# Moving weights in the expert blocks and four dense output buffers, in a fused attention and mixture-of-experts kernel

## The chip, the cores and the metric

The kernel runs on one core of one Trainium2 chip, in one launch. The metric is the time on the device in microseconds (us). The kernel before the change took 663.98 us, the median of three runs (662.36 to 671.49).

A core has engines with instruction streams of their own: TensorE (PE in the profile, with its weight loads shown as PEld), VectorE (DVE), ScalarE (ACT), GpSimd (POOL) and SyncE (SP). They meet through semaphores. TensorE multiplies a *stationary* operand, loaded beforehand, with a *moving* operand that streams through the array, and writes to PSUM; other engines copy results from PSUM to SBUF. Transfers between SBUF and device memory run on DMA queues, which SyncE, ScalarE or GpSimd issue.

## What is computed

The reference in short, with the shapes of this case:

```python
# attention: q, k, v are [8, 8, 576, 64]
rel = pos[:, None] - pos[None, :]
scores = q @ k.T / 8 + slopes[h] * -abs(rel)         # ALiBi
scores = where((rel >= 0) & (rel < 128), scores, -1e9)
attn = softmax(scores)
x = (attn @ v)                                        # as [4608, 512]: 8 batches x 576 tokens
# mixture of experts on x
y_dense = relu(x @ w1_dense) @ w2_dense               # all weights 512 x 512
logits = x @ w_gate                                   # 8 experts
e = argmax(logits); gate = softmax(logits)[e]
y_moe = gate * (relu(x @ w1[e]) @ w2[e])              # one expert for each token
out = y_dense + y_moe                                 # [4608, 512], float32
```

## The kernel before

The program is one list of steps `n`. In the first 48 steps it does attention, three steps for each unit of one batch and four heads. Three steps behind, the attention rows are transposed (`flip`); then come the gate and the dense layer of each batch. Each token's row (x in bf16, its gate weight, its token number) is scattered to `xs_dram`, sorted by expert, and its dense result to `ys_dram`. From step 50 on, 43 *expert blocks* of 128 rows each load such rows back, apply the expert's two layers, add the dense result and scatter to `out`.

The order within a step is the order in which the engines get their instructions:

```python
while jm < NB:
    for f in gates.pop(n, []): f()          # gate_a, gate_b, gate_c, gate_d, routing
    lo = scores(u, pr)                      # TensorE scores, ScalarE exponentials p32
    if n - 2 in norms: norms.pop(n - 2)()   # VectorE: normalize, xf and xrow
    flip(*steps[n - 3])                     # TensorE transposes tp; ScalarE copies xT, xTb
    ...                                     # what is due later is put into gates and items
    for f in todo[:1]: f()                  # one item of the dense layer
    norms[n - 1] = attend(*steps[n - 1])    # TensorE: p @ v
    for f in todo[1:]: f()                  # the other items
    ...                                     # loads and casts of the next q, k, v
    lo()                                    # VectorE: low parts of p
    if n > NS + 1: block(jm); jm += 1
    n += 1
```

`tp`, `lp` (gate), `lg`, `pc`, `hp` and `yp` (dense) all take turns in one pair of PSUM buffers, with the tag `misc` in the pool `psum_m`. The dense layer:

```python
def dense1(b, c, hf):                       # hf: half of the 576 tokens, 288 each
    hp = psum_m.tile([P, 512], F32, name="hp", tag="misc")
    ...                                     # 4 matmuls of 288 columns
    nc.scalar.activation(out=hT[...], in_=hp[:, 0:HF], func=ACT.Relu)

def dense2(b, t):                           # t: one of five tiles of tokens
    yp = psum_m.tile([P, 512], F32, name="yp", tag="misc")
    ...                                     # 4 matmuls of 512 columns
    yt = xpool.tile([P, DM], F32, name="yt", tag="yt")     # xpool: 2 buffers
    nc.scalar.copy(out=yt[:rows, :], in_=yp[:rows, :])
    nc.gpsimd.indirect_dma_start(out=ys_dram[:, :], ..., in_=yt...)
```

The expert blocks:

```python
def fetch(j):                               # xr, yr: 4 buffers each
    ...                                     # SyncE loads xr from xs_dram, yr from ys_dram
def turn_x(j):
    ...                                     # 4 transposes of xr into xps; VectorE copies to xT
def layer1(j):
    hp = psum_h.tile([P, 4, P], F32, name="hpm", tag="hpm")
    for c in range(4):
        for kc in range(4):                 # weights stationary, 128 tokens moving
            nc.tensor.matmul(out=hp[:, c, :],
                lhsT=w_all[:, bass.DynSlice(er, 1), 0, kc, c * P : c * P + P],
                rhs=xT[:, kc, :], start=(kc == 0), stop=(kc == 3))
    nc.scalar.activation(out=hT, in_=hp, func=ACT.Relu)
def layer2(j):
    for c in range(4):                      # hT stationary, 512 weight columns moving
        nc.tensor.matmul(out=y, lhsT=hT[:, c, :],
            rhs=w_all[:, bass.DynSlice(er, 1), 1, c, :], start=(c == 0), stop=(c == 3))
    nc.vector.scalar_tensor_tensor(out=yo, in0=y, scalar=xr[:, GC : GC + 1], in1=yr,
        op0=ALU.mult, op1=ALU.add)          # gate weight times y, plus the dense result
    nc.gpsimd.indirect_dma_start(out=out[:, :], ..., in_=yo[:, :])   # token numbers from xr
def block(j):
    if j == 0: turn_x(0); layer1(0); turn_x(1)
    layer1(j + 1); turn_x(j + 2); layer2(j); fetch(j + 4)
```

## Time and profile before

The profile is of one execution with a span of 669.2 us.

| | busy us | share of the span | instructions |
|---|---|---|---|
| TensorE matmuls | 492.8 | 74% | 4378 |
| TensorE weight loads | 287.9 | 43% | 4424 |
| VectorE | 286.2 | 43% | 567 |
| ScalarE | 241.3 | 36% | 412 |
| GpSimd | 148.2 | 22% | 193 |

The mean granted clock of TensorE was 0.832 of full speed; 83.03 MB went through the DMA queues, 124 GB/s on average.

The lines in the prediction come from these views. *Stretches*: for each stretch of time, its length, then the busy time of each engine with the number of its instructions, the granted clock, the share of the DMA engines' time and their rate. *Waits*: who waited for whom, the sum in us, how many times, and the longest. An engine name with q is the engine's queue, such as SPq for SyncE's. *Timeline*: start, duration, engine, line of the kernel, operation and tiles (written <- read), and in brackets how long the engine was idle before, and what ended that.

L numbers are lines of the kernel: L373 and L384 are the scores, L394 the exponentials, L447 attend, L463 the normalization, L497 the copies xT and xTb, L513 the gate's matmuls, L642 and L649 the dense first layer and its ReLU, L658, L666 and L667 the dense second layer, its copy yt and its scatter, L845 the loads of a block, L860 and L866 the transposes xps and their copy, L881 and L889 the expert's first layer and its ReLU, L897 the second layer, L905 its sum, L913 the scatter to out.

### The profile page before, as it was taken

The page shows a single profiled execution, that of the slowest core. Times are in us where ns is not written, and L with a number is a line of the kernel's source. Part 1 is how long each engine was busy: PE and PEld are TensorE (multiplying, and loading weights), DVE is VectorE, ACT ScalarE, POOL GpSimd, SP SyncE. Part 2 cuts the span into 40 slices and gives each one's busy share as a digit, 9 for nine tenths or more (in the row PEclk, how much of TensorE's full clock was granted, in tenths as well). Part 3 has the DMA queues.
Part 4 walks back from the last instruction along what each step waited for, and adds up shares of the span by engine and source line. Part 5 has one row for each costly group of instructions (what it writes and reads, how often), then busy time and mean ns, then how long its engine had stood idle before and what let it go on. Part 6 is the DMA issues. An engine that isn't in the chain of part 4 may idle for free.

```text
span 669.2 us, 12798 instructions
## 1 busy us (share of the span) xinstructions
PE 492.8 (74%) x4378; PEld 287.9 (43%) x4424; DVE 286.2 (43%) x567; ACT 241.3 (36%) x412; POOL 148.2 (22%) x193
## 2 busy tenths in 40 slices
PE   1454877577677787675766687798877999999994
PEld 0343564254354454343534455344433444544442
DVE  4675764464563563644716744021142222222221
ACT  2433754463563563453635644221210111111110
POOL 4000012313303303213213212213411121222221
PEclk9996868787887887987968988797877787787887
DMA  8635663616636535625444121523474443444340
GB/s 171 161 109 140 149 144 100 189 38 158 189 61 153 164 75 132 171 66 144 110 129 104 19 85 41 162 79 103 160 227 151 149 128 113 132 126 142 122 147 21
DMA packets 87695, 83.03 MB, mean 124 GB/s; under 512 B 43603, under 2 KB 74323, under 8 KB 87636
## 3 DMA queue, kind: packets, MB, share of 16 engines
q1 hardware_dynamic: 69560, 48.76, 25.5%
q0 software_dynamic: 17680, 33.12, 19.6%
q8 instruction: 41, 0.67, 0.4%
q10 hardware_dynamic: 396, 0.33, 0.2%
q14 instruction: 18, 0.15, 0.1%
HBM read 64.79 MB, written 28.66 MB: 140 GB/s over the span
## 4 chain that ended last, share of the span: by engine, by line
issue 32%; PE 20%; DMA 18%; ACT 8%; POOL 8%; DVE 7%; another core or an unknown queue 3%; SPq 2%; POOLq 1%; ACTq 0%; DVEq 0%
DMA ys_dram<-yt,slot 11%; POOL out_dram L913 5%; PE hpm L881 4%; DMA qraw<-in_q_dram 4%; PE sq L373 3%; ACT p L394 3%; POOL xs_dram L599 3%; PE hp L642 3%; DVE plo L413 2%; PE sq L384 2%; PE lp L513 2%; DMA vf<-in_v_dram 2%; PE y L897 1%; ACT yt L666 1%
## 5 line engine op out<-in xcount | busy, mean ns | idle before, releaser
L881 PE MATMUL hpm<-xTm,w_all 128*128 128x128 bf16 x688 | 137.2, 240 | 12.0 <-DVE xTm L866 4.2
L413 DVE TENSOR_TENSOR plo<-p 128x1024 bf16<-128x1024 f32 (+1 forms) x96 | 82.9, 905 | 99.7 <-ACT p L394 99.1
L881 PEld LDWEIGHTS <-w_all 128*128 x688 | 68.9, 106 | 91.9 <-issue 33.3
L394 ACT ACTIVATE p<-sq 128x1024 f32<-128x1024 f32 (+1 forms) x96 | 69.2, 775 | 66.0 <-PE sq L384 65.9
L447 PE MATMUL ax<-vf,p 128*128 128x65 bf16 (+1 forms) x576 | 72.1, 212 | 26.2 <-DVE xf L463 26.2
L889 ACT ACTIVATE hTm<-hpm 128x512 bf16<-128x512 f32 x43 | 25.7, 597 | 174.7 <-PE hpm L881 174.7
L447 PEld LDWEIGHTS <-p 128*128 128x128 bf16 (+1 forms) x1152 | 70.1, 112 | 36.1 <-DVE xf L463 28.1
L866 DVE COPY xTm<-xps 128x512 bf16<-128x512 bf16 x43 | 18.2, 424 | 145.8 <-PE xps L860 136.9
L913 POOL DMA_INDIRECT out_dram<-yo,xr x43 | 42.1, 979 | 173.8 <-DVE yo L905 159.0
L447 PE MATMUL ax<-vf,plo 128*128 128x65 bf16 (+1 forms) x576 | 71.3, 209 | 2.8 <-DVE plo L413 2.8
L642 PE MATMUL hp<-xTb,w_all 128*128 128x288 bf16 x256 | 48.1, 317 | 34.1 <-ACT xTb L497 32.6
L447 PE MATMUL ax<-vl,p 128*128 128x64 bf16 (+1 forms) x576 | 71.5, 208 | 1.1 <-DVE vl L195 1.1
L667 POOL DMA_INDIRECT ys_dram<-yt,slot x40 | 41.6, 1040 | 112.1 <-ACT yt L666 107.4
L513 PE MATMUL lp<-xT,wg_pad 128*32 128x288 f32 x128 | 31.0, 585 | 45.4 <-ACT yt L666 21.8
L447 PEld LDWEIGHTS <-plo 128*128 128x128 bf16 (+1 forms) x576 | 61.9, 111 | 4.4 <-DVE plo L413 4.4
L897 PE MATMUL y<-w_all,hTm 128*128 x154 | 58.2, 502 | 1.9 <-issue 1.1
L658 PE MATMUL yp<-w_all,hTd 128*128 128x512 bf16 (+1 forms) x147 | 43.6, 408 | 19.6 <-ACT yt L666 13.1
L373 PE MATMUL sq<-mask,ident_b 128*128 128x512 bf16 (+1 forms) x177 | 47.9, 395 | 12.0 <-DVE mask L249 9.3
L649 ACT ACTIVATE hTd<-hp 128x288 bf16<-128x288 f32 x64 | 27.2, 425 | 72.0 <-remote 44.9
L599 POOL DMA_INDIRECT xs_dram<-xrow,slot x40 | 38.4, 961 | 61.4 <-DVE xrow L591 51.3
L905 DVE SCALAR_TENSOR_TENSOR yo<-y,xr,yr 128x512 f32<-128x512 f32 x43 | 32.3, 750 | 38.5 <-PE y L897 36.0
L666 ACT COPY yt<-yp 128x512 f32<-128x512 f32 (+1 forms) x40 | 23.6, 591 | 68.7 <-DMA ys_dram<-yt,slot 55.1
(139 smaller groups left out, 560.8 us busy)
## 6 DMA issues: line engine op xcount, KB each, us to landing
yr<-ys_dram SPq DMA_DIRECT2D x43, 256.0 KB
kraw<-in_k_dram SPq DMA_DIRECT2D x16, 576.0 KB
qraw<-in_q_dram SPq DMA_DIRECT2D x66, 128.0 KB
vf<-in_v_dram SPq DMA_DIRECT2D x64, 128.0 KB
w_all<-in_moe_w_dram POOLq DMA_DIRECT2D x16, 512.0 KB
xr<-xs_dram SPq DMA_DIRECT2D x43, 130.0 KB
ys_dram<-fill_y SPq DMA_DIRECT2D x8, 256.0 KB
xs_dram<-fill_x SPq DMA_DIRECT2D x8, 130.0 KB
```

The lines of the kernel that those rows point to most:

```text
L373: nc.tensor.matmul(out=sq[g // 2][:, g % 2, 0:tot], lhsT=ident_b, rhs=rhs, start=True, stop=False,)
L394: nc.scalar.activation(out=p32[:, :, 0:tot], in_=sq[i][:, :, 0:tot], func=ACT.Exp, scale=SCALE,)
L413: nc.vector.tensor_tensor(out=plo[:, :, 0:tot], in0=p32[:, :, 0:tot], in1=phi[:, :, 0:tot], op=ALU.subtract,)
L447: nc.tensor.matmul(out=ax[:rows, i, o0 : o0 + w], lhsT=lhs, rhs=rhs, start=(n == 1), stop=(n == 3 * len(kl)),)
L513: nc.tensor.matmul(out=lp[r0 : r0 + 32, 0:HF], lhsT=wg_pad[:, 2 * (u % HQ) + c, :], rhs=cur["xT"][:, c, hf * HF : (hf + 1) * HF], start=Tr ...
L599: ins = nc.gpsimd.indirect_dma_start(out=xs_dram[:, :], out_offset=bass.IndirectOffsetOnAxis(ap=slot[:rows, t : t + 1], axis=0), in_=xrow. ...
L642: nc.tensor.matmul(out=hp[:, 0:HF], lhsT=w_all[:, E, 0, kc, c * P : c * P + P], rhs=xTb[:, kc, hf * HF : hf * HF + HF], start=(kc == 0), s ...
L658: nc.tensor.matmul(out=yp[:rows, :], lhsT=hT[:, c, t * P : t * P + rows], rhs=w_all[:, E, 1, c, :], start=(c == 0), stop=(c == 3),)
L667: ins = nc.gpsimd.indirect_dma_start(out=ys_dram[:, :], out_offset=bass.IndirectOffsetOnAxis(ap=slots[b][:rows, t : t + 1], axis=0), in_=y ...
L881: nc.tensor.matmul(out=hp[:, c, :], lhsT=w_all[:, bass.DynSlice(er, 1), 0, kc, c * P : c * P + P], rhs=xT[:, kc, :], start=(kc == 0), stop ...
L897: nc.tensor.matmul(out=y, lhsT=hT[:, c, :], rhs=w_all[:, bass.DynSlice(er, 1), 1, c, :], start=(c == 0), stop=(c == 3),)
L913: ins = nc.gpsimd.indirect_dma_start(out=out[:, :], out_offset=bass.IndirectOffsetOnAxis(ap=xr.bitcast(I32)[:, TC : TC + 1], axis=0), in_= ...
```

## The change

It has these parts.

- **Expert blocks**: in the first layer x becomes the stationary operand and the weights move, 512 columns at a time. The result then has the tokens on the partitions, so that the gate weight can be applied in the ReLU as a scale for each row (it is positive, and the second layer is linear), and h must be transposed for the second layer (`turn_h`). It is meant to need fewer instructions on TensorE.
- **Dense output**: `yt` has four buffers. The dense layer runs in two token parts, tiles 0 and 1 (256 tokens), then tiles 2 to 4 (320 tokens), each through both layers, so that `hTd` is smaller.
- **Transposes first**: `flip` comes ahead of the scores in each step. The gate's matmuls become items beside the dense ones, and the gate's later parts are due a step or more earlier.
- **Space**: `fill_y` goes (the padding rows of `ys_dram` are filled from `fill_x`, in two pieces for each row instead of four), the constant `ut_f` takes a buffer of the probabilities, `ge` is bf16.

The core of the diff; cuts are marked with dots.

```diff
-    def gate_a(u):
+    def gate_a(u, hf):
...
-        for hf in range(2):
-            lp = psum_m.tile([P, 512], F32, name="lp", tag="misc")
+        lp = psum_m.tile([P, 512], F32, name="lp", tag="misc")
...
+    DT = [(0, 2), (2, NT)]
+
     def dense1(b, c, hf):
-        HF = S // 2
+        c0, c1 = DT[hf][0] * P, min(DT[hf][1] * P, S)
+        HF = c1 - c0
...
-        yt = xpool.tile([P, DM], F32, name="yt", tag="yt")
+        yt = xpool.tile([P, DM], F32, name="yt", tag="yt", bufs=4)
...
-        return [one[0:2], one[2:4], one[4:6], one[6:8], two[0:2], two[2:5]]
+        return [one[0:2], one[2:4], two[0:2], one[4:6], one[6:8], two[2:5]]
...
-        hp = psum_h.tile([P, 4, P], F32, name="hpm", tag="hpm")
+        hp = psum_h.tile([P, FF], F32, name="hpm", tag="hpm")
+        for kc in range(4):
+            nc.tensor.matmul(
+                out=hp,
+                lhsT=xT[:, kc, :],
+                rhs=w_all[:, bass.DynSlice(er, 1), 0, kc, :],
+                start=(kc == 0),
+                stop=(kc == 3),
+            )
+        hr = mpool.tile([P, FF], BF16, name="hr", tag="hr")
+        nc.scalar.activation(out=hr, in_=hp, func=ACT.Relu, scale=xr[:, GC : GC + 1])
+        st[("g", j)] = (hr, er)
+
+    def turn_h(j):
+        hr, er = st.pop(("g", j))
+        hps = psum_t.tile([P, 4, P], BF16, name="hps", tag="xps")
         for c in range(4):
-            for kc in range(4):
-                nc.tensor.matmul(
...
+            nc.tensor.transpose(
+                out=hps[:, c, :], in_=hr[:, c * P : (c + 1) * P], identity=ident_b
+            )
         hT = mpool.tile([P, 4, P], BF16, name="hTm", tag="hTm")
-        nc.scalar.activation(out=hT, in_=hp, func=ACT.Relu)
+        nc.scalar.copy(out=hT, in_=hps)
...
-        nc.vector.scalar_tensor_tensor(
-            out=yo, in0=y, scalar=xr[:, GC : GC + 1], in1=yr, ...
+        nc.vector.tensor_tensor(out=yo, in0=y, in1=yr, op=ALU.add)
...
             turn_x(1)
+        turn_h(j)
         if j + 1 < NB:
             layer1(j + 1)
...
-            for f in gates.pop(n, []):
-                f()
+            if 0 <= n - 3 < NS:
+                flip(*steps[n - 3])
+                ...                         # gate_a and gate_b, gate_c become items
             lo = None
             if n < NS:
                 u, pr = steps[n]
                 lo = scores(u, pr)
             if n - 2 in norms:
                 norms.pop(n - 2)()
-            if 0 <= n - 3 < NS:
-                flip(*steps[n - 3])
-                ...
+            for f in gates.pop(n, []):
+                f()
```

## The prediction

> **What bounds the kernel now.** I read the busy times by stretches first, because one average over 669 us hides that the program has two halves: attention with gates and dense layer (to about 427 us), then 43 expert blocks.

> ```profile
> core 0: us, PE busy (x) PEld busy (x) DVE busy (x) ACT busy (x) POOL busy (x), PEclk, DMA share, GB/s
> ...
> 200.00:250.00 50.00, 37.55 (x420) 23.44 (x424) 25.93 (x48) 25.72 (x44) 13.44 (x15) 0.81 0.52 131
> ...
> 520.00:560.00 40.00, 38.41 (x200) 19.51 (x202) 9.83 (x17) 5.37 (x9) 7.82 (x8) 0.80 0.40 125
> ```

> One batch of attention lasts about 51 us (step starts in the timeline: 184.2, 235.1, 288.7). TensorE works in 37.55 of 50 us there: a quarter is waiting, so the waits decide that half. In the expert stretch TensorE works in 38.41 of 40 us while VectorE, ScalarE and the transfers stay under half: TensorE alone decides there. The waits view says what the attention half waits for:

> ```profile
> ACT yt L666 <- DMA ys_dram<-yt,slot: 55.1, 21, 4.9
> ACT hTd L649 <- remote: 44.9, 7, 7.2
> PE hp L642 <- ACT xTb L497: 32.6, 26, 2.5
> ...
> PE lp L513 <- ACT yt L666: 21.8, 11, 4.5
> ...
> PE lp L513 <- ACT hTd L649: 17.6, 5, 4.5
> ...
> PE yp L658 <- ACT yt L666: 13.1, 6, 2.6
> ```

> ScalarE cannot empty a dense result, because both yt buffers still feed scatters (55.1 us). TensorE then finds no free PSUM buffer of the pair named misc: 21.8 + 13.1 us. It also waits 32.6 us for the copies xTb, which stand behind the exponentials on ScalarE. The chain of waits agrees: it puts 11% of the span on the dense scatter, its largest transfer share. For the other half, two expert blocks in the timeline:

> ```profile
> 561.16 0.98 POOL L913 DMA_INDIRECT out_dram<-yo,xr  x1 [4.21 <-DVE yo L905]
> ...
> 562.62 0.38 PE L860 MATMUL xps<-ident_b,xr 128*128 128x128 bf16 x4
> ...
> 562.88 0.60 ACT L889 ACTIVATE hTm<-hpm 128x512 bf16<-128x512 f32 x1 [4.22 <-PE hpm L881]
> 563.04 0.42 DVE L866 COPY xTm<-xps 128x512 bf16<-128x512 bf16 x1 [2.16 <-PE xps L860]
> ...
> 563.74 3.71 PE L881 MATMUL hpm<-xTm,w_all 128*128 128x128 bf16 x16
> 563.91 0.75 DVE L905 SCALAR_TENSOR_TENSOR yo<-y,xr,yr 128x512 f32<-128x512 f32 x1 [0.44 <-PE y L897]
> 564.00 0.33 SPq L845 DMA_DIRECT2D xr<-xs_dram  x1
> ...
> 564.93 0.98 POOL L913 DMA_INDIRECT out_dram<-yo,xr  x1 [2.79 <-DVE yo L905]
> ```

> The 16 first-layer matmuls take 3.71 us even at full clock (the windows view has 1.00 there): 0.224 us from start to start, though each moves 128 columns. A second-layer matmul moves 512 columns and starts every 0.215 us at full, every 0.427 us at half clock. The first layer is bound by the issuing of four instructions for each matmul (two address computations, weight load, matmul), not by the array. From the 11th output scatter (512.55) to the 42nd (659.84) lie 31 blocks of 4.75 us.

> [...] Here the clock does change in steps of 3.41 us, but it falls to 0.50 in stretches where the windows view has TensorE busy 1.00. [...] Here the next xr load starts 1.86 us after the scatter instruction before it ended (562.14 to 564.00).

> **The change, part by part.**

> *Expert blocks, TensorE.* Removed per block: 16 weight loads and 16 matmuls with the weights stationary, 3.6 us by the spacing above. Added: 4 matmuls that move 512 columns, 4 x 0.215 = 0.86 us, and 4 transposes, 0.38 us as for xps. A block is then 0.38 (hps) + 0.86 (layer 1) + 0.38 (xps) + 0.86 (layer 2) = 2.5 us at full clock. [...] I expect the clock near 1.0 in this stage.

> *Expert blocks, the other engines.* ScalarE gets a second evacuation: 0.60 + about 0.60 = 1.2 us a block. VectorE's output loses its multiplication and becomes a plain sum, 0.69 us as for the same shape at L463. Both stay under half of any period below. The new round trip (layer 1, ReLU, transpose, copy, layer 2) spans two steps: between hps and layer 2 TensorE has 0.86 + 0.38 us, against 0.60 plus some 0.3 of signals.

> *Expert blocks, the loop through memory.* There are still four xr buffers, and one is refilled only when its output scatter has landed:

> ```profile
> SPq L845 <- DMA out_dram<-yo,xr: 89.3, 28, 4.6
> ```

> From the timeline: output sum to scatter start 563.91 to 564.93, 1.02 us; scatter start to the next xr load 561.16 to 564.00, 2.84; that load to its last packet 564.00 to 565.68, 1.68, and up to 2.5 when it meets the yr load; then the transposes and layer 2 to the next output sum, 0.38 + 0.86 + 0.2. Together 7.0 to 7.8 us. The transposes run two blocks ahead and there are four buffers, so this is the length of two periods: a period is at least 3.5 to 3.9 us. Today's 4.75 hides it; with 2.5 us of TensorE it becomes the bound. I take 3.7: 31 x (4.75 - 3.7) = 33 us saved.

> *First blocks (427 to 512 us).* Ten blocks run there between the last batch's gates and dense layer, and one gap: TensorE waits 5.0 us for xr while SyncE issues the padding writes. TensorE bound, each block is worth 3.6 - 1.24 = 2.4 us less; but the loop limits them too and the gap stays. I take 20 us.

> *Dense layer.* Four yt buffers, with the scatters in groups of two and three and two steps between the groups, leave no scatter to wait for: of 21.8 + 13.1 = 35 us of TensorE idle time nearly all goes. The two parts of 256 and 320 tokens move the same columns as two of 288.

> *Transposes first.* xT and xTb are copied ahead of the exponentials, while TensorE still makes the scores. Of 32.6 us I expect two thirds, 22 us, to go; the gate's first half now follows its transposes closely and will wait in their stead. Against this I set 5 us of new waits. Attention: 35 + 22 - 5 = 52 us.

> *The rest* (no fill_y, a bf16 ge, the mask constant in a probability buffer) is off the path: under 0.5 us.

> Sum: 33 + 20 + 52 = 105 us, of which I keep 102, for three stages that can't all pay fully. 664 - 102 = 562 us.

> **Rivals.** (a) *TensorE alone still bounds the blocks*: 2.5 us at full clock, or 3.0 at today's 0.82. Then 31 x 2 = 62 us instead of 33, and about 530 us in all. Against it speaks the loop above, which no part of the change shortens by more than 0.1 us. (b) *The round trip over ScalarE becomes the bound*: if transposes wait for the ReLU in each step, a block is about 4.3 us; the stage then gives 14 us and the total is near 585. For it: xps and hps share one pair of PSUM buffers. Against: the order of instructions leaves 1.2 us of other TensorE work in each of the two waits. (c) *The attention waits are only exchanged.* Without the scatter waits a batch is 42 to 44 us; transfers, at a share of 0.52 today, would go to about 0.61, and the first 100 us show 0.60 to 0.64 with waits for q. Also the 44.9 us of hTd (a source that the profile does not tell; it falls together with the scatter of xs) stay. If half of the 52 us come back, the total is near 590. (d) *The dense scatters were hidden anyway*: the chain of waits has them with 11%, so I give this little.

> **Range and chances.** Attention alone may give 20 to 65 us, the blocks with their start 35 to 85. Both at their low end: about 609; both high: 514; neither corner is likely, and the estimate lies nearer to the good end of attention. I take 535 to 602. Every part of the sum points the same way and the threshold of 2% is 13 us, so faster 0.96, same 0.03, slower 0.01.

> **What would show it.** In the new profile: waits of yt for the ys_dram scatter near zero, and xTb waits a third of 32.6; batches of 42 to 44 us; blocks of 3.7 us, with TensorE busy under 80% of that stage, clock above 0.95, and TensorE or its loads waiting for the DMA of xr. If the blocks are shorter than 3.3 us, my loop is wrong; if they stay above 4.2 with waits for ScalarE, rival b is right; if the batches stay above 47 us, rival c. What would make the total wrong most easily is the attention half, where I removed waits one by one although each may uncover another.

## The result and the profile after

The changed kernel took **537.9 us** (537.49 to 539.59, three runs) against 663.98: a ratio of 0.8076 with a 95% interval of 0.7997 to 0.8156, 126 us less. The prediction of 562.0 had counted on 102; the result lies inside its range, near the fast end. How the 126 us are made up differs from the sum.

The windows view cuts both kernels at the first scores of the second and of the sixth batch, so each line holds four whole batches of attention, with the same 1,680-odd recorded TensorE matmuls. Before, then after, then after in the expert stretch; the columns are the stretch, its length, each engine's busy time, the granted clock, the share of the transfers, and GB/s:

```profile
core 0: us, PE busy (x) PEld busy (x) DVE busy (x) ACT busy (x) POOL busy (x), PEclk, DMA share, GB/s
106.90:314.90 208.00, 145.79 (x1682) 92.05 (x1696) 106.62 (x189) 106.63 (x186) 52.42 (x62) 0.82 0.50 126
```
```profile
101.70:248.30 146.60, 127.76 (x1687) 82.76 (x1697) 107.37 (x189) 106.81 (x185) 57.44 (x63) 0.97 0.73 181
...
450.00:490.00 40.00, 26.62 (x159) 13.15 (x161) 11.17 (x20) 12.73 (x20) 9.84 (x10) 0.91 0.49 152
```

A batch went from 208.0 / 4 = 52.0 us to 36.7. TensorE's idle time fell from 62.2 us in four batches to 18.8, 10.8 us less in each. But its *busy* time fell as well, by 18.0 / 4 = 4.5 us a batch for the same work, and the clock rose from 0.82 to 0.97. The prediction has nothing for that, and so its batches of 42 to 44 us were too long. In the expert stretch TensorE is now busy 26.6 of 40 us.

The waits view after, by total, count and longest:

```profile
PEld L864 <- DMA xr<-xs_dram: 70.5, 34, 8.4
...
PE hp L647 <- ACT hTd L654: 6.9, 9, 1.1
...
PE lp L510 <- DVE sl L585: 5.1, 6, 1.0
...
PE tp L488 <- ACT yt L670: 3.6, 5, 1.0
...
PE tp L488 <- ACT hTd L654: 3.3, 7, 0.5
...
PE hp L647 <- ACT xTb L495: 0.3, 1, 0.3
```

The waits of TensorE for yt (21.8 + 13.1 us before) have shrunk to 3.6, those for xTb (32.6) to 0.3, and that of hTd for an untold source (44.9) is not in the view at all (2.7 us of the kind are left at other tiles); nor is there a wait of yt for the scatter to `ys_dram` (55.1). The new ones sum to about 19 us, the yt wait included. At the top stands the wait that the prediction named for the blocks: the transposes' weight load, waiting for xr.

Two blocks of the timeline after show the loop through memory:

```profile
450.41 0.69 DVE L920 TENSOR_TENSOR yo<-y,yr 128x512 f32<-128x512 f32 x1 [0.44 <-PE y L912]
...
451.38 0.98 POOL L921 DMA_INDIRECT out_dram<-yo,xr  x1 [3.67 <-DVE yo L920]
...
454.23 0.33 SPq L849 DMA_DIRECT2D xr<-xs_dram  x1
...
456.32 0.23 PEld L864 LDWEIGHTS <-xr 128*128 128x128 bf16 x4 [1.48 <-DMA xr<-xs_dram]
456.33 0.40 PE L864 MATMUL xps<-ident_b,xr 128*128 128x128 bf16 x4 [0.99 <-DMA xr<-xs_dram]
...
456.56 1.03 PE L912 MATMUL y<-w_all,hTm 128*128 x4
...
457.63 0.69 DVE L920 TENSOR_TENSOR yo<-y,yr 128x512 f32<-128x512 f32 x1 [0.44 <-PE y L912]
```

Sum to scatter 0.97 us, scatter to the next load of its buffer 2.85, load to transposes 2.09, transposes to the output sum two blocks on 1.31: 7.22 us for two periods. This turn is one of the shortest. Over 27 turns in that trace the means are 0.97, 3.49, 2.24 and 1.40, together 8.1 us. From the 11th output scatter (402.2) to the 42nd (525.6) a block takes 123.4 / 31 = 3.98 us.

### The profile page after: what moved, and what is told of

It is laid out like the page before. It is cut to its first block, busy times and chain, and to the rows that moved or that the text cites. A ratio compares the mean times of both kernels' runs of the same rounds, so it can differ in the third digit from the quotient of the medians.

```text
span 535.8 us, 11040 instructions
## 1 busy us (share of the span) xinstructions
PE 378.4 (71%) x4043; PEld 228.6 (43%) x4080; DVE 283.1 (53%) x566; ACT 271.3 (51%) x455; POOL 158.0 (29%) x193
## 3 DMA queue, kind: packets, MB, share of 16 engines
q0 software_dynamic: 17680, 33.12, 24.3%
## 4 chain that ended last, share of the span: by engine, by line
PE 30%; issue 25%; DVE 16%; ACT 8%; DMA 8%; POOL 7%; SPq 3%; POOLq 1%; another core or an unknown queue 0%; DVEq 0%; ACTq 0%
PE ax L445 7%; DVE plo L411 7%; POOL out_dram L921 7%; PE hp L647 4%; PE yp L662 4%; DMA vf<-in_v_dram 4%; PE sq L382 3%; ACT p L392 3%; PE lp L510 3%; PE sq L371 2%; DVE xf L461 2%; PE tp L488 2%; ACT qT L182 2%; SPq L167 2%; DVE qs L175 2%
## 5 line engine op out<-in xcount | busy, mean ns | idle before, releaser
L870 DVE COPY xTm<-xps 128x512 bf16<-128x512 bf16 x43 | 18.2, 424 | 123.4 <-PE xps L864 106.7
L904 ACT COPY hTm<-hps 128x512 bf16<-128x512 bf16 x43 | 25.2, 586 | 88.3 <-PE hps L900 86.7
L864 PE MATMUL xps<-ident_b,xr 128*128 128x128 bf16 x172 | 18.6, 236 | 54.0 <-DMA xr<-xs_dram 54.0
L885 PE MATMUL hpm<-w_all,xTm 128*128 x162 | 48.5, 417 | 5.1 <-DVE xTm L870 3.6
L912 PE MATMUL y<-w_all,hTm 128*128 x167 | 47.4, 406 | 4.4 <-ACT hTm L904 3.9
L647 PE MATMUL hp<-xTb,w_all 128*128 128x256 bf16 (+1 forms) x256 | 42.1, 293 | 11.7 <-ACT hTd L654 6.9
L371 PE MATMUL sq<-mask,ident_b 128*128 128x512 bf16 (+1 forms) x183 | 39.6, 327 | 11.4 <-DVE mask L249 9.2
L893 ACT ACTIVATE hr<-hpm,xr 128x512 bf16<-128x512 f32 x43 | 29.6, 687 | 27.7 <-PE hpm L885 20.2
L864 PEld LDWEIGHTS <-xr 128*128 128x128 bf16 x172 | 12.0, 105 | 74.1 <-DMA xr<-xs_dram 70.5
L920 DVE TENSOR_TENSOR yo<-y,yr 128x512 f32<-128x512 f32 x43 | 29.7, 691 | 22.8 <-PE y L912 22.8
L654 ACT ACTIVATE hTd<-hp 128x256 bf16<-128x256 f32 (+1 forms) x64 | 26.1, 412 | 23.7 <-PE hp L647 19.8
```

The source lines that it names most:

```text
L371: nc.tensor.matmul(out=sq[g // 2][:, g % 2, 0:tot], lhsT=ident_b, rhs=rhs, start=True, stop=False,)
L647: nc.tensor.matmul(out=hp[:, 0:HF], lhsT=w_all[:, E, 0, kc, c * P : c * P + P], rhs=xTb[:, kc, c0:c1], start=(kc == 0), stop=(kc == 3),)
L864: nc.tensor.transpose(out=xps[:, kc, :], in_=xr.bitcast(BF16)[:, kc * P : (kc + 1) * P], identity=ident_b,)
L885: nc.tensor.matmul(out=hp, lhsT=xT[:, kc, :], rhs=w_all[:, bass.DynSlice(er, 1), 0, kc, :], start=(kc == 0), stop=(kc == 3),)
L912: nc.tensor.matmul(out=y, lhsT=hT[:, c, :], rhs=w_all[:, bass.DynSlice(er, 1), 1, c, :], start=(c == 0), stop=(c == 3),)
```

## The experiments

They ran in three sets, each set on one chip. The kernel before took 668.6, 630.5 and 631.3 us beside them, so the chips aren't alike and differences are taken within a set where possible. The theories: the blocks are bound by the loop of refills (L); in attention the dense buffers and the order of transposes each took away waits (W), and the faster clock came on top (C). The rivals are those of the prediction, and each expectation says what its letters stand for where they differ.

### Set 1 (before: 668.63 us): parts undone one at a time

**Two dense output buffers.** In the changed kernel:

```diff
-        yt = xpool.tile([P, DM], F32, name="yt", tag="yt", bufs=4)
+        yt = xpool.tile([P, DM], F32, name="yt", tag="yt", bufs=2)
```

> The changed kernel with two yt buffers instead of four; all else as changed. Theory W (the waits for the dense scatters were what the four buffers removed): in the new item order only the last tile of each batch has to wait for a scatter, some 5 to 6 us for each of 8 batches, so 575 to 585 us, and the waits view shows yt waiting 40 us or more for ys_dram. Theory C (most of the attention gain came from the higher TensorE clock and from the transposes): under 550 us.

Measured 554.81 us (ratio to before 0.8311, 0.824 to 0.8381), 17 us above the first measurement of the changed kernel. Neither number was met. With the layer split in two parts, the scatters already lie apart, and two buffers cost only half of what the waits before had suggested: yt waits 28.3 us for `ys_dram` in this profile, where W wanted 40 or more.

**Transposes late.** The `flip` of the changed kernel goes back behind the scores and norms:

```diff
             if 0 <= n - 3 < NS:
-                flip(*steps[n - 3])
                 ...
             if n - 2 in norms:
                 norms.pop(n - 2)()
+            if 0 <= n - 3 < NS:
+                flip(*steps[n - 3])
```

> The changed kernel with the transposes (flip) back behind the scores and the normalization; the rest of the order as changed. Theory W: the dense and gate matmuls wait for xT and xTb behind the exponentials again, 3 to 4 us a batch, so 560 to 570 us, TensorE waiting about 25 us for the copies at L495. Theory O (the moved gates and the item order did it, not the place of flip): within 5 us of 538.

Measured 573.2 us (0.8595, 0.8518 to 0.8672): 35 us, more than W's 22 to 32. The waits for xTb are back (16.5 + 12.1 us in its waits view for hp and yp), and the clock of the whole program is 0.916 instead of 0.930. Not all of it is the order of the copies: this profile also has 22.7 us of waits of ScalarE (ltsb, 4 times) for the untold source, beside 2.7 in that of the changed kernel. Theory O falls all the same; set 3 gives the cleaner number.

**Old expert blocks.** The changed kernel with the 16 small matmuls, the ReLU over `hpm` and the multiplying output sum of before, without `turn_h`.

> The changed kernel with the first expert layer as before: weights stationary, no second transpose, the gate weight in VectorE's sum. Theory W: blocks of 4.7 us instead of 3.98, so 538 + 33 x 0.75 + about 10 for the first blocks: 570 to 580 us; the granted clock in the block stage falls back to about 0.81 while TensorE is busy for 95% of it. Rival (the clock follows busy time): a clock above 0.9 in that stage, because TensorE is busier than in the changed kernel.

Measured 574.66 us (0.856, 0.8484 to 0.8637): the new blocks are worth 37 us, not the 53 of the sum. A block takes 4.74 us, and the clock in the stage is back at 0.82 with TensorE busy 37.3 of 40 us (the line stands in the last section), beside 0.91 at 26.6 of 40 us in the changed kernel, so the rival falls: the clock does not follow the busy time that the profile books.

**Five buffers for the loads.**

```diff
-    AHEAD = 3          # and bufs=4 for xr and yr
+    AHEAD = 4          # and bufs=5 for xr and yr
```

> The changed kernel with five xr and yr buffers instead of four, and blocks fetched one block earlier. Theory L (a block period is the refill loop of 7.96 us shared by two blocks): with five buffers the loop is shared by three, 2.65 us, about the 2.5 us of TensorE work, so 33 x 1.25 = 41 us less: 495 to 505 us, TensorE over 90% busy in the blocks. Rival D (the transfers themselves are the limit): 657 KB a block at 2.65 us would be 250 GB/s, and if the queues give only some 200 GB/s a period stays above 3.2 us: 512 to 530 us.

Measured 500.47 us (0.7458, 0.7395 to 0.7521), within the total of L, and the limit of rival D falls: the transfers run at 202 GB/s from 410 to 450 us here, and at 241 with six buffers (last section). The blocks take 2.95 us (402.6 to 494.0 for 31) and not 2.65, and TensorE is busy 82% of that stretch, not over 90: the loop is shared by three, but it has grown longer (below). One more buffer gives as much as the whole rewriting of the blocks did.

### Set 2 (before: 630.54 us): the loop to both sides, and two combinations

**Three buffers, six buffers** (the same edit, with 3 and 2, and with 6 and 5).

> The changed kernel with three buffers for xr and yr and the loads two blocks ahead. Loop (L): with four buffers a refill has two periods, and they lasted 2 x 3.98 = 7.96 us; with three it has one, so a block takes about 8 us and the kernel 33 x 4 = 130 us more, about 670 us. TensorE or ScalarE as the bound (O): a buffer less changes little, 538 to 560 us.

> The changed kernel with six buffers for xr and yr and the loads five blocks ahead. Loop (L): 7.96 / 4 = 2.0 us would be left of the loop, below TensorE's 2.5 us, so TensorE is the bound: blocks of 2.5 to 2.7 us, 488 to 500 us in all, and hardly a wait for xr. If another thing than the number of buffers holds the blocks with five of them at 2.9 (transfers, GpSimd's scatters), six change nothing: 498 to 503 us.

Three: 672.52 us, one run. It meets the number, but on a faster chip: it is 151 us above the changed kernel there (set 3), 31 x (8.06 - 4.12) = 122 for the later blocks and the rest for the first ones. Six: 464.82 us (0.734, 0.729 to 0.7391), the fastest of all; 0.734 of the 664 us of the first measurement would be 487, just under what was expected. TensorE waits 7.7 us for xr instead of 54.0. The profiles of five and six buffers are of the slowest of four runs each (505.96 and 470.25 us). The block periods, scatter to scatter, settle it:

| buffers | periods for one refill | block, us | product, us |
|---|---|---|---|
| 3 | 1 | 8.06 | 8.06 |
| 4 | 2 | 3.98 (4.12 in set 3) | 7.96 (8.24) |
| 5 | 3 | 2.95 | 8.85 |
| 6 | 4 | 2.51 | 10.04 |

The product is the length of the loop as long as the loop binds: about 8 us for three and four buffers, longer with five. What grows is the term from scatter to the next load: 2.80, 3.49, 3.66 and 4.15 us in the mean with three to six buffers, while the DMA engines are busy 0.24, 0.49, 0.67 and 0.76 of the stretch. That denser transfers cause it fits, and isn't shown apart. With six buffers a loop of 8.85 us would allow 8.85 / 4 = 2.2, and another thing binds. The timeline with six buffers shows which, from one turn of hps to the next:

```profile
432.58 0.39 PE L900 MATMUL hps<-ident_b,hr 128*128 128x128 bf16 x4
...
432.99 1.02 PE L885 MATMUL hpm<-w_all,xTm 128*128 x4
...
433.85 0.39 PE L864 MATMUL xps<-ident_b,xr 128*128 128x128 bf16 x4
...
434.07 1.03 PE L912 MATMUL y<-w_all,hTm 128*128 x4
...
434.94 0.39 PE L900 MATMUL hps<-ident_b,hr 128*128 128x128 bf16 x4
```

The groups follow each other almost without a gap: TensorE is the bound, at 434.94 - 432.58 = 2.36 us here. (The length of a matmul group contains its modelled end; what counts is from start to start.) This was rival (a): it needs two buffers more than the change has.

**The new blocks alone, in the kernel before.** The exchange of `old_blocks`, the other way round.

> The kernel before with the new expert blocks alone. If the parts add up, what the old blocks cost inside the changed kernel (574.7 - 537.9 = 37 us) comes off here: 627 to 633 us, with blocks of about 4.0 us and attention batches of 51 to 53 us as before. If the blocks gain more where the attention stays slow (transfers less crowded), below 620.

Measured 596.82 us (0.9437, 0.939 to 0.9484), 34 us less than before, and its blocks take 4.08 us (458.5 to 585.1). The absolute numbers were set for a slower chip, so a time below 620 says nothing; the difference is near the 37 us of set 1. The blocks are worth about the same in both surroundings.

**The old dense layer in the changed kernel**: one part of 576 tokens, two yt buffers, five scatters together.

> The changed kernel with the dense layer of the kernel before: one part of all 576 tokens, two yt buffers, all five scatters close together; the transposes still come first and the new blocks stay. Waits one by one (W), as predicted: the yt waits return, 35 us, 570 to 577 us. Clock (C): the waits of the scatter also let the clock fall, which lengthens the rest of each batch; batches of 44 us or more, clock under 0.9 in attention, 585 to 600 us. Depth alone (D): the two token parts do nothing by themselves, and it equals the changed kernel with two yt buffers, 553 to 557 us.

Measured 559.16 us (0.8859, 0.8828 to 0.8889). The bounds were written for a changed kernel of 538 us; on a like chip it took 521.7 (set 3), so the old dense layer costs 37 us. That is W's amount (32 to 39 above the changed kernel), not C's (47 or more) nor D's (15 to 19). But W meets it partly by luck, as four whole batches show:

```profile
100.93:263.05 162.12, 137.31 (x1698) 88.77 (x1696) 106.79 (x189) 106.78 (x185) 54.36 (x62) 0.89 0.66 162
```

The changed kernel of set 3 needs 136.5 us for them. Of the 25.6 us more, 13.1 are idle time and 12.5 busy time of TensorE at a clock of 0.89 for 0.97. TensorE's waits for yt are 14.5 us in the whole run (11.5 before yp, 3.0 before lg), not 35. The clock is under 0.9, as C has it; the batches of 40.5 us are not its 44.

### Set 3 (before: 631.27 us): the changed kernel on a chip of the faster kind

**Both kernels again.**

> The kernel before, profiled once more, because its time was 630.5 us beside the last four kernels and 664 to 669 us in the earlier sets. If the waits of hTd for a source that the profile does not tell (44.9 us in the first profile) are the cause (R), a time near 630 us comes without them and with a sixth step of each batch of about 9 us, and a time near 665 us with them and with 12 to 14 us. If the cause is another (O), the waits stand in both, or all steps are longer alike.

> The changed kernel once more, beside the kernel before in the same set. With the waits for the untold source in the kernel before (time near 665 us) the ratio is that of the first measurement, 0.80 to 0.815. Without them (near 630 us) the change has some 25 to 35 us less to gain: 510 to 522 us, ratio 0.81 to 0.83.

The kernel before took 635.69 us in its profiled run, and its waits view has no line for the untold source; hTd waits for its matmul alone, and the waits for yt and xTb stand as in the first profile:

```profile
ACT yt L666 <- DMA ys_dram<-yt,slot: 55.7, 22, 5.4
...
ACT hTd L649 <- PE hp L642: 45.1, 42, 3.2
...
PE hp L642 <- ACT xTb L497: 34.1, 27, 2.5
...
PE lp L513 <- ACT yt L666: 23.0, 11, 5.0
...
PE yp L658 <- ACT yt L666: 14.5, 8, 2.4
...
PE yp L658 <- ACT xTb L497: 3.7, 10, 0.4
```

The sixth step of a batch (scores to scores) takes 8.6 to 9.3 us instead of 12 to 14. So R holds as far as two profiles of the kernel before can tell: the one with that wait is of a run of 670.9 us, the one without of 635.69. The other profiles agree. All six of the first measurement and of set 1 have waits for an untold source (67.4 us before, 2.7 after, 1.1 to 42.6 in set 1), the eight of sets 2 and 3 none. The changed kernel took 521.74 us, ratio 0.8285 (0.8213 to 0.8356): 109.5 us less here, within what was expected.

**The new dense part alone, in the kernel before** (two token parts, four buffers, items a step later, and the space that they need).

> The kernel before with the new dense part alone: two token parts, four yt buffers, items one step later; transposes late and old expert blocks. The changed kernel with late transposes took 573.2 us beside 668.6 us for the kernel before, and the old blocks cost 37 us in it, so 610 us is left if the parts add up: 58 us off where the kernel before shows the untold waits (ratio 0.905 to 0.92), and 25 to 35 us off, those of the yt waits, where it does not (0.945 to 0.96). If the waits are only exchanged (rival c), under 15 us off.

Measured 583.03 us (0.9239, 0.9171 to 0.9307): 48 us, more than the 25 to 35 us of the waits. The three profiles of this set in the windows view, four whole batches each as above, say why (before, dense part alone, changed):

```profile
101.20:288.30 187.10, 136.97 (x1683) 90.45 (x1698) 107.75 (x189) 106.10 (x185) 52.18 (x63) 0.85 0.57 141
```
```profile
100.40:251.20 150.80, 126.53 (x1691) 86.07 (x1698) 106.09 (x189) 105.19 (x184) 53.34 (x63) 0.95 0.72 176
```
```profile
100.80:237.30 136.50, 124.79 (x1687) 81.84 (x1697) 107.36 (x189) 106.28 (x185) 59.37 (x63) 0.97 0.77 193
```

TensorE's idle time in four batches is 50.1, 24.3 and 11.7 us, its busy time 137.0, 126.5 and 124.8. The dense part takes 25.9 us of waiting away and 10.4 us of busy time; the order of the transposes then 12.6 and 1.7. Busy time times clock comes to 116, 120 and 121 us, nearly the same work, so it is the clock that shortens it. Nearly all that the clock gives comes with the first of the two. In the waits view of the dense part alone, TensorE's waits for yt (23.0 + 14.5 us) are down to 0.2, and those for xTb (34.1 + 3.7) are nearly untouched:

```profile
PE hp L645 <- ACT xTb L495: 27.6, 25, 2.5
...
PE yp L660 <- ACT xTb L495: 8.6, 12, 0.7
...
PE hp L645 <- ACT yt L668: 0.2, 1, 0.2
```

**One dense part, three yt buffers**, otherwise the changed kernel.

> The changed kernel with the old dense layer in one part, but with three yt buffers [...]. If it is the number of buffers that counts (N), most of the difference between the old dense layer with two and the new one with four goes: within 12 us of the changed kernel in this set. If the split in two token parts, which draws the scatters apart, is needed too (S), it stays 25 us or more above the changed kernel, near the old dense layer with two (559 us, 0.886 of the kernel before).

Measured 538.37 us (0.8523, 0.8461 to 0.8586): 16.6 us above the changed kernel, between the two theories. The third buffer gives back 21 of the 37 us; the other 17 belong to the fourth buffer and the split together. Four buffers with the undivided layer were not run. With two buffers the split can be told: 37 us above the changed kernel without it, 17 with it (set 1, so on another chip). Buffers and split each give something.

## Why the prediction was right, and by which steps not

In set 3 the parts can be added up: blocks 34 us (from set 2, where before took the same time), dense layer 48, and what is left of 109.5 for the transposes, 28.

**Expert blocks and the loop: mechanism right, one term mis-sized.** The loop binds, not TensorE (rival a) and not ScalarE (rival b): more buffers alone make the blocks 2.95 and 2.51 us, fewer make them 8.06. Of "a period is at least 3.5 to 3.9 us ... I take 3.7" the term that failed is scatter start to the next xr load: 2.84 us was read from one turn while TensorE still was the bound (2.99 is the mean there), and it is 3.49 on the mean of the changed kernel. The others hold (0.97 for 1.02, 2.24 inside 1.68 to 2.5, 1.40 for 1.44). The 31 blocks then saved 31 x (4.75 - 3.98) = 24 us instead of 33. The first ten blocks gave 10 instead of 20 in the first pair: from the 1st to the 11th output scatter 73.7 us before, 63.8 after. In the pair of set 3 they gave 18 (76.4 and 58.7), near the 20, and the 31 others 31 x (4.74 - 4.12) = 19. The gap around the padding writes did stay, and grew: between the 7th and 8th scatter after lie 14.1 us, 10.4 between the 9th and 10th before. The new work of TensorE was sized well, 2.5 us predicted against 2.36 in the timeline with six buffers. TensorE is busy 67% of the stretch, as predicted under 80%; its clock of 0.91 to 0.96 is a little under the predicted 0.95 and above, which was the author's estimate.

**Dense layer: the waits right, the clock missing.** "Nearly all goes" of the 35 us is what happened, and the runs make it a cause (rival d falls): undoing the dense part alone costs 37 us, doing it alone gains 48. The difference to 35 is in large part the busy time above, 10.4 us in four batches, at a clock of 0.95 for 0.85; of what undoing it costs, busy time is half. That no part of the attention sum had a term for the clock is the step that failed. It was in reach in part: the prediction's own lines have a clock of 0.81 in a stretch where TensorE waits a quarter of the time, and it names stretches at 0.50 that are booked as busy throughout, so the clock was not a constant to leave out. That it rises as these waits go is shown by the runs alone.

**Transposes first: both terms too small.** Expected were 22 us of waits gone and 5 new, 17 net. What happened: the waits for xTb went as a whole (32.6 to 0.3), and more new ones came, about 19 us in the first profile after with the rest of yt, 13.4 in that of set 3. The part measures 28 us as what is left over in set 3; its profiles put 26.0 of them ahead of the first output scatter (349.5 us with the dense part alone, 323.5 with all). The 35 us of set 1 hold untold waits too. The 28 us also hold the moved gate, which no run took alone.

**The untold wait: assumed to stay, and gone.** The prediction kept the 44.9 us of hTd. They aren't in the changed kernel's profile, nor in that of the kernel before on the chip of set 3, and in set 1 such waits came back with the late transposes. The first pair gained 126 us and the second 109.5, and before differs between the two by 33. So some 17 us of the surplus of 24 are particular to the first chip, where before lost 33 us and after 16. Rival c (waits only exchanged, 590 us) falls: batches of 36.7 and 34.1 us, far below its 47, with transfers at a share of 0.73 to 0.77 where 0.61 was expected; TensorE's waits for the casts of newly loaded q hardly grew (sq for qT 7.2 us after, 6.1 before).

So the total was right partly by luck, two errors against each other: the blocks gave 34 to 37 for 53, the attention about 90 for 52 on the first chip and 76 on the later one.

## What to carry to other kernels

Where a buffer is refilled through memory, add up its loop from the timeline and divide it by the periods that the number of buffers leaves; once the engine's own work is shorter, one buffer more can be worth as much as the rewriting (37 us each here). Read the loop's terms with a margin: from scatter to the next load it was 2.80 us at blocks of 8.06 us here, and 4.15 at 2.51. And when a change removes TensorE's waits, count the work that runs faster if the clock rises too: for the dense part here 2.6 us a batch at 0.95 instead of 0.85, beside 6.5 us of waiting.

## What the runs showed of the hardware that was not expected

**Equal busy time, another clock.** In the changed kernel with the old blocks, and with six buffers, the windows view of an expert stretch has:

```profile
450.00:490.00 40.00, 37.32 (x199) 19.41 (x203) 9.39 (x16) 4.78 (x8) 8.28 (x9) 0.82 0.42 124
```
```profile
410.00:450.00 40.00, 37.19 (x253) 19.60 (x251) 17.70 (x32) 20.23 (x32) 15.66 (x16) 1.00 0.79 241
```

```profile
543.00:544.00 1.00, 0.97 (x9) 0.71 (x9) 0.00 (x0) 0.14 (x1) 0.00 (x0) 0.73 0.44 168
544.00:545.00 1.00, 1.00 (x5) 0.44 (x4) 0.42 (x1) 0.46 (x1) 0.00 (x0) 0.50 0.08 16
545.00:546.00 1.00, 1.00 (x6) 0.46 (x4) 0.07 (x1) 0.00 (x0) 0.00 (x0) 0.50 0.53 128
546.00:547.00 1.00, 1.00 (x10) 0.69 (x7) 0.69 (x1) 0.00 (x0) 0.04 (x1) 0.57 0.26 32
547.00:548.00 1.00, 0.87 (x5) 0.38 (x4) 0.00 (x0) 0.00 (x0) 0.94 (x1) 1.00 0.73 236
```

What differs between the blocks, old and new, is the columns moved: 16 of the old block's 24 matmuls and transposes are first-layer matmuls of 128 columns, and the new one has 4 of 512 and 4 transposes in their place. In the first profile before, 352 of 420 of these matmuls start 0.22 to 0.24 us after the last at full clock, and 100 of 225 at half clock, where 97 start only 0.10 to 0.12 us after it. So it is not the array that holds them to 0.22; for each of the 688 there are two register instructions and a weight load in the trace. Nor is busy time a measure of columns: the profile books 0.216 us (the median) for one of these matmuls of 128 columns and 0.379 for one of 512. An estimate from the shapes is 4608 columns for an old block and 5120 for a new one. Over 31 blocks that is 635 columns per us with three buffers, 972 with the old blocks, 1286, 1735 and 2040 with four, five and six buffers. The clocks are 0.65, 0.85, 0.94, 0.98 and 1.00, in the same order; the busy shares, 52, 94, 64, 82 and 93%, are not. That it is the columns remains the reading that fits; no run varied them alone.

**One kernel, 664 or 631 us.** The kernel before, unchanged, took 664 to 669 us in two sets and 631 in two others. The traces put most of the difference into one step in six of attention (12 to 14 us or 8.6 to 9.3). The first one of before also shows what the untold source of hTd is: the semaphore that it waits for is raised by TensorE's instructions alone, all 524 that raise it. Four matmuls that this profile books as ended between 204.02 and 205.96 us have their semaphore raised at 207.59, 209.00, 209.06 and 209.11, and hTd starts at 209.08. Whether TensorE ended so late or only its signal came late, and why those chips show it, is open.
